# Retention and two MLPs on one core: in-weight stores moved to block 1, ring requests one by one, evacuations ahead of units

## The chip, the cores and the metric

The kernel runs on 1 core of one Trainium2 chip. The metric is the device time of one execution in microseconds (us). TensorE (PE) does the matmuls into PSUM, ScalarE (ACT) and VectorE (DVE) evacuate PSUM and convert operands, GpSimd (POOL) takes a few elementwise operations, and SyncE (SP) issues almost all DMAs. Every engine takes its own instructions in the order in which the program wrote them.

## The reference

```python
# retention, B=4, H=8, S=768, D=64
for t in range(S):
    state = gamma * state + outer(k[t], v[t])
    y[t] = (1 / sqrt(D)) * q[t] @ state
x = y.transpose(0, 2, 1, 3).reshape(3072, 512)
# first MLP, 512 -> 2048 -> 512
h = maximum(x @ w_in, 0.0)
x = h * h @ w_out
# second MLP, 512 -> 1536 -> 512
xn = x / sqrt(mean(x * x) + 1e-6) * rms_g
g = xn @ w_gate
out = (g / (1 + exp(-g)) * (xn @ w_val)) @ w_out
```

The weights come as 64-bit floats, everything else as 32-bit floats.

## The kernel before, in words

**Arithmetic.** A 32-bit operand is held as a high part (rounded to the matmul's own format) and a low part (what the rounding left). A product is three matmuls: high by high, high by low, low by high (`mm3`, lines 243 to 246, and `proj`, line 269). Where a large product allows it, a scheme of seven products in place of eight is used (P1 to P7): `Out` for the output projections, `pair` for the second MLP's first layer. Its seven weight combinations are "units" of 512 KB (128 partitions by 1024 values).

**Stages.** The 3072 tokens are six tiles of 512. Tile 0 goes through `block1(0, ...)`, tile 1 through `block1(1, ...)` (called block 1 below): for each of 16 steps f a projection with the in-weight f, squared ReLU, and the product with the out-weight f. Tiles 2 and 3 go through the first paired phase: `in_phase(xs, ...)` (line 1064; per step f two half steps t = 0, 1, one per tile, each a projection into `ph[t]`, evacuated by ACT with L394 and L395), then `out_1.run`. Tiles 4 and 5 do the same in the second paired phase (`in_phase(xs2, ...)`, line 1144, and `out_2.run`). Then the second MLP runs in three super-steps s of two tiles, each six pairs (`pair`, line 633) and an `out_3.run`.

**Retention beside it.** The chunks of the retention are computed in "visits" (`visit`, `after_visit`): every second step of block 1 and of the first paired phase a visit computes one chunk, its result goes through `xh` (ACT) and `xl` (DVE) into the operand of a later tile, and the loads of `vnt`, `knt`, `qnt`, `kTt` for the chunk after the next are issued on SP. POOL scales `qnt` and `vnt`.

**Weight conversion.** `tick` (line 221) converts one 128x512 piece of 64-bit weights per call: ACT's L203 (`magnitude`) writes a buffer `f` of three, one piece ahead; DVE's L208 and L209 (`convert`) finish it, and `fetch_to` loads the raw piece (512 KB) that comes three later. The next tick's `finish2` stores a gate or value piece to DRAM (`wq<-f`, L181, 256 KB), or splits an out-weight piece and leaves the store of its units to `later`. `more_steps(W2_SOON)` at step 15 of block 1 opens the first 25 of the second MLP's 36 pieces; the rest follow in the second paired phase. `stores()` issues what was appended to `later`.

**Ring and units.** In the second paired phase and in the output projections weights come through a ring of seven buffers, refilled in the order of `stream`. The in-weights of the second paired phase are read back from `wi`, which the first paired phase stores (line 1042). The first seven loads are issued together behind step 13 (lines 1055 to 1058). In super-step 0 of the second MLP the units are made in place: `make_unit(n, k)` (line 592) reads quarters of the gate and value weights (`quarter`, loaded from `wq`), casts with ACT and DVE into `own[k]`, loads the next pair's quarter into the one just freed, and appends the unit's store `wu` to `later`; the next `make_unit` begins with `stores()`.

**Order of a pair.** `both(k, acc, ...)` is a product of 12 matmuls. P1, P6, P7 and P4 go into `main` (`ph` or `pb`, by turns), P5 and P3 into `pa`, P2 into `pr`. `take` copies an accumulator with ACT (L111 in the trace), `add` adds it with DVE (L107), `act2` is SiLU on ACT (L628) and a product on DVE (L629). P7 writes `main` only after `take(p6, main)`, and P4 only after `add(p5, main)`. The units are made between these steps, in the order in which the program has them.

Of the kernel before, what the change touches and what calls it, by code (L numbers as in the profile page):

```python
# [9 lines left out]
F32 = mybir.dt.float32  # L10
F32R = mybir.dt.float32r
# [28 lines left out]
AHEAD = 5  # L40
EARLY = 24
MORE_AT = 15
W2_SOON = 25
OPEN_AT = 12
PREP_IN = 10

P2, P1, P5, P6, P7, P3, P4 = range(7)
# [10 lines left out]
def retention_then_two_mlps(  # L58
    ctx: ExitStack, tc: tile.TileContext, qT, kT, kn, vn, w1i, w1o, w2g, w2v, w2o, rmsg, tri, qdec, vdec, sdec, dec, out
):  # L60
    nc = tc.nc
# [10 lines left out]
    wi = [dram.tile([128, 2, 512], F32, name=f"wi{f}") for f in range(NF1)]  # L72
# [11 lines left out]
    def slot(name, dt=F32):  # L84
        return wp.tile([128, 2, 512], dt, tag="w", name=name)
# [13 lines left out]
    def split(dst_h, dst_l, src, el):  # L99
        nc.scalar.copy(dst_h, src)  # L100
        low(el, dst_l, src, dst_h)

    def sub(out_, a, b):
        nc.vector.tensor_tensor(out=out_, in0=a, in1=b, op=ALU.subtract)

    def plus(out_, a, b):
        nc.vector.tensor_tensor(out=out_, in0=a, in1=b, op=ALU.add)  # L107

    def take(dst, acc):
        for m in range(2):  # L110
            nc.scalar.copy(dst[:, m], acc[m])  # L111

    def add(dst, acc):
        for m in range(2):
            plus(dst[:, m], acc[m], dst[:, m])

    def units(t):
        return t.rearrange("p i (l n) -> p i l n", l=2)

    W = {}  # L120
# [17 lines left out]
    def keep_units(to, f, w):  # L138
        q, r, c = f // 4, f % 4 // 2, f % 2
        for k, h in ((P1, 0),) if r == 0 else ((P2, 0), (P4, 1)):  # L140
            nc.sync.dma_start(units(to[q][k])[:, c], w.bitcast(F32)[:, :, h * HALF:(h + 1) * HALF])
# [73 lines left out]
    later = []  # L215

    def stores():
        while later:
            later.pop(0)()
# [19 lines left out]
    def more_steps(n):  # L239
        upto[0] = min(upto[0] + n, len(steps))  # L240
        fetch_to(at[0] + 2)
# [128 lines left out]
    ring, own, stream, ring_at = [], [], [], [0]  # L370

    def load_unit(i):
        if i < len(stream):
            nc.sync.dma_start(ring[i % 7].bitcast(F32), stream[i])

    def next_unit():
        i = ring_at[0]
        ring_at[0] += 1
        return ring[i % 7]

    def unit_done():
        load_unit(ring_at[0] + 6)
# [204 lines left out]
    def load_quarters(n, *which):  # L587
        if n < NPR:
            for r, h in which:
                nc.sync.dma_start(quarter[r, h], w2q[n][:, r, h])  # L590

    def make_unit(n, k):
        stores()
        if n >= NPR:
            return
        a11, a12, a21, a22 = (quarter[r, h] for r in range(2) for h in range(2))
        u = units(own[k])

        def put(src):
            split(u[:, :, 0, :], u[:, :, 1, :], src, nc.vector)  # L600

        if k == P5:
            plus(mix, a21, a22)
            put(mix)
            sub(a21, a11, a21)
        elif k == P6:
            sub(mix, mix, a11)
            put(mix)
            sub(a11, a12, mix)
            load_quarters(n + 1, (0, 1))  # L610
        else:
            put({P1: a11, P2: a12, P3: a11, P7: a21, P4: a22}[k])
            if k in (P3, P7, P4):
                load_quarters(n + 1, {P3: (0, 0), P7: (1, 0), P4: (1, 1)}[k])
        later.append(lambda: nc.sync.dma_start(wu[n][k], own[k].bitcast(F32)))

    def product(acc, u, k, m, start):
        xh, xl = X[k]
        for c in range(2):
            wc = slice(c * 128, (c + 1) * 128)  # L620
            mm3(
                acc, u[:, m, 0, wc], u[:, m, 1, wc], xh[:, c], xl[:, c], start and c == 0, c == 1,
                skip_group_check=True,
            )

    def act2(g, v, a):
        t = tp.tile([128, TB], F32, tag="t0", name="t")
        nc.scalar.activation(t, g, AF.Silu)  # L628
        nc.vector.tensor_tensor(out=a, in0=v, in1=t, op=ALU.mult)  # L629
# [3 lines left out]
    def pair(s, n, first, second):  # L633
        p1, p5, p6 = part[:3]
        a0, a1 = (act[n % 2][t][n // 2] for t in range(2))
        main = (ph, pb)[n % 2]

        def both(k, acc, start):
            u = units(own[k] if s == 0 else next_unit())
            for m in range(2):  # L640
                product(acc[m], u, k, m, start)
            if s:
                unit_done()
            elif n == NPR - 1:
                load_unit(ORDER.index(k))

        def make(n, k):
            if s == 0:
                make_unit(n, k)

        both(P2, pr, True)
        make(n, P7)
        both(P1, main, True)
        make(n, P3)
        make(n, P4)
        take(p1, main)
        add(p1, pr)
        first()
        act2(p1[:, 0], p1[:, 1], a0[:, 0])
        both(P5, pa, True)  # L660
        take(p5, pa)
        make(n + 1, P2)
        make(n + 1, P1)
        both(P6, main, False)
        take(p6, main)
        second()
        make(n + 1, P5)
        both(P7, main, False)
        make(n + 1, P6)
        add(p5, main)  # L670
        act2(p5[:, 0], p5[:, 1], a1[:, 1])
        both(P3, pa, False)
        add(p6, pa)
        act2(p6[:, 0], p6[:, 1], a1[:, 0])
        both(P4, main, False)
        act2(main[0], main[1], a0[:, 1])

    with tc.manual_schedule():
# [299 lines left out]

        def keep_out(f):
            keep_units(uo, f, W[("o", f)])  # L980

        xs = []
        made = all_units()
# [7 lines left out]
        def early1(f):  # L991
            if f == MORE_AT:
                more_steps(W2_SOON)
            if f > MORE_AT:
# [44 lines left out]
        def after1(f, t):  # L1039
            nonlocal at_chunk  # L1040
            if t == 0:
                nc.sync.dma_start(wi[f], W[("i", f)].bitcast(F32))
                stores()
                tick()
                if f and f % 2 == 0:
                    decay_v(at_chunk + 1, nc.gpsimd)
                    decay_q(at_chunk + 2, nc.gpsimd)
                    at_chunk += 1
            elif f % 2:
                kv = visit(at_chunk, pa, True)  # L1050
                after_visit(at_chunk, sink2(at_chunk), kv)
            elif f % 2 == 0:
                tick()
            make_some()
            if f == 13 and t == 0:
                ring.extend(slot(f"ring{n}", F32R) for n in range(7))
                for n in range(7):
                    load_unit(n)
            if (f, t) in ((14, 1), (15, 0), (15, 1)):
                n = (f - 14) * 2 + t - 1  # L1060
                out_1.hi(n)
                out_1.lo(n)
# [44 lines left out]
        out_2 = Out(NQ, act, pair2)  # L1107
# [15 lines left out]
        def after2(f, t):  # L1123
            if t == 1:
                unit_done()
            if f < OPEN_AT and t == 0:
                stores()
                tick()
            if t == 1 and 3 <= f < 7:
                if f == 3:  # L1130
                    yn.extend(big(f"yn{t_}") for t_ in range(2))
                h, t_ = ((1, 0), (0, 0), (0, 1), (1, 1))[f - 3]
                nc.sync.dma_start(yn[t_][:, 2 * h:2 * h + 2, :], ys[t_][:, 2 * h:2 * h + 2, :])
            if f == 5 and t == 0:
                prep[0] = prep_x(0, {(h, t_): yn[t_][:, 2 * h:2 * h + 2, :] for h in range(2) for t_ in range(2)}, True)
                next(prep[0])
            if (f, t) in ((14, 1), (15, 1)):
                out_2.hi(f - 14)
                out_2.lo(f - 14)

        def w_of2(f):
            return next_unit()

        in_phase(xs2, w_of2, after2, between2)
        out_2.hi(2)
        next(prep[0], None)
        while back:
            background()
# [62 lines left out]
        for s in range(NS):  # L1211
# [5 lines left out]
            for p in range(NPR):  # L1217
# [7 lines left out]
                def first():  # L1225
                    background()
                    if p == 0:
                        background()
                    if p == NPR - 1:
                        for n in range(2):  # L1230
                            out_3.hi(n)
                            out_3.lo(n)
                        next(coming, None)
                        next(coming, None)

                def second():
                    if p == 0 and due:
                        sums(pb[1])
                        background()
                    if p == NPR - 1:  # L1240
                        out_3.hi(2)
                        next(coming, None)
                        next(coming, None)
# [86 lines left out]
```

## Time and profile before

| | before |
|---|---|
| median of three runs | 1146.3 us (1145.23 to 1146.66) |
| the profiled execution's own time | 1146.94 us |
| its span, first to last instruction | 1145.2 us |
| PE busy | 1112.7 us (97%) |
| DVE busy | 713.8 us (62%) |
| ACT busy | 561.0 us (49%) |
| POOL busy | 46.0 us (4%) |
| mean granted clock of PE | 0.993 |

Busy time is the union of an engine's instructions; issuing a DMA doesn't count. "Idle before" an instruction is put down to whatever ended it last. The DMA share is the mean busy share of the core's 16 DMA engines. A matmul of 512 columns shows 0.39 us, as matmuls overlap. Times in the rows are us from the span's start. The stages lie at: block 1 from 143 to 242, first paired phase to 374, `out_1` to 453, second paired phase to 541, `out_2` to some 618, super-step 0's pairs from there to beyond 720.

### The profile page before, as it was taken

The numbers are of one execution on the slowest core, as the hardware profiler recorded it, in microseconds if no ns is written. First come the engines' busy times: TensorE is split into PE (matmuls) and PEld (weight loads), VectorE is DVE, ScalarE is ACT, GpSimd is POOL, SyncE is SP. The second block draws the span as 40 slices with busy tenths as digits, with TensorE's granted clock in tenths as the row PEclk, the third lists the DMA queues.
The fourth block names the chain that finished last, engine by engine and source line by source line (L and its number), as shares of the span: only waits on it lengthen the run. The fifth ranks groups of instructions, "written<-read, shape, count | busy, mean of one in ns | idle before, by whom it ended". The sixth has DMA issues, their size and how long they took to land.

```text
span 1145.2 us, 15762 instructions
## 1 busy us (share of the span) xinstructions
PE 1112.7 (97%) x5962; PEld 909.0 (79%) x5962; DVE 713.8 (62%) x962; ACT 561.0 (49%) x918; POOL 46.0 (4%) x39
## 2 busy tenths in 40 slices
PE   9999999999977999999999999999999999999998
PEld 7788888887765788888888787888888888888887
DVE  6877337767842774442977676888343788333585
ACT  4776445557644542665546444454323454323442
POOL 0000122112110000000000000000000000000000
PEclk9999999999999899999999999999999999999999
DMA  9943445699999467874556568666656666555563
GB/s 359 342 157 112 148 129 195 222 368 340 331 390 368 159 208 259 299 254 153 203 193 239 216 237 322 224 205 231 211 200 242 234 209 232 211 195 194 193 212 118
DMA packets 96411, 266.68 MB, mean 233 GB/s; under 512 B 10168, under 2 KB 27472, under 8 KB 96336
## 3 DMA queue, kind: packets, MB, share of 16 engines
q1 hardware_dynamic: 95760, 265.47, 65.3%
q8 instruction: 47, 0.77, 0.3%
q10 hardware_dynamic: 576, 0.20, 0.1%
q14 instruction: 28, 0.23, 0.1%
HBM read 190.65 MB, written 74.99 MB: 232 GB/s over the span
## 4 chain that ended last, share of the span: by engine, by line
PE 85%; DMA 7%; DVE 3%; ACT 3%; issue 1%; SPq 0%; ACTq 0%; DVEq 0%
PE ph L276 17%; PE ph L244 8%; PE ph L245 8%; PE ph L246 8%; PE pa L244 7%; PE pa L246 6%; PE pa L245 6%; PE pb L244 4%; PE pb L246 4%; PE pb L245 4%; PE pr L245 3%; PE pr L244 3%; PE pr L246 3%; DMA up<-wps 2%; DMA wi<-w_i 1%; PE pr L773 1%
## 5 line engine op out<-in xcount | busy, mean ns | idle before, releaser
L276 PE MATMUL ph<-xh,w_i 128*128 128x512 f32 x512 | 167.7, 395 | 11.6 <-ACT act L394 10.3
L435 ACT CAST o<-act 128x1024 fp32r<-128x1024 f32 x101 | 105.7, 1052 | 99.4 <-PE ph L246 44.0
L97 DVE TENSOR_TENSOR o<-act,o 128x1024 fp32r<-128x1024 f32 x101 | 122.6, 1220 | 35.6 <-ACT o L435 35.6
L276 PEld LDWEIGHTS ph<-xh,w_i 128*128 128x128 f32 x512 | 96.7, 189 | 35.9 <-ACT act L394 12.9
L276 PE MATMUL ph<-xl,w_i 128*128 128x512 f32 x256 | 100.0, 392 | 0.0
L244 PE MATMUL ph<-o,ring 128*128 128x512 f32 x228 | 88.7, 389 | 0.0
L245 PE MATMUL ph<-o,ring 128*128 128x512 f32 x228 | 88.7, 389 | 0.0
L246 PE MATMUL ph<-o,ring 128*128 128x512 f32 x228 | 88.7, 389 | 0.0
L276 PE MATMUL ph<-xh,ring 128*128 128x512 f32 x256 | 79.3, 390 | 0.0
L628 ACT ACTIVATE t<-part 128x512 f32<-128x512 f32 x54 | 34.1, 632 | 67.3 <-DVE part L107 67.3
L107 DVE TENSOR_TENSOR part<-pr,part 128x512 f32<-128x512 f32 x36 | 24.9, 692 | 65.7 <-ACT part L111 65.7
L244 PE MATMUL ph<-xop,ring 128*128 128x512 f32 x144 | 57.2, 397 | 2.9 <-ACT part L111 2.0
L111 ACT COPY part<-ph 128x512 f32<-128x512 f32 x50 | 29.1, 588 | 62.7 <-PE ph L246 62.6
L244 PE MATMUL pb<-xop,ring 128*128 128x512 f32 x144 | 56.4, 392 | 2.1 <-ACT part L111 1.5
L245 PE MATMUL ph<-xop,ring 128*128 128x512 f32 x144 | 56.8, 394 | 0.0
L246 PE MATMUL ph<-xop,ring 128*128 128x512 f32 x144 | 56.6, 393 | 0.0
L276 PEld LDWEIGHTS ph<-xl,w_i 128*128 128x128 f32 x256 | 48.5, 189 | 9.7
L276 PEld LDWEIGHTS ph<-xh,ring 128*128 128x128 f32 x256 | 48.1, 188 | 10.1 <-issue 0.2
L246 PE MATMUL pb<-xop,ring 128*128 128x512 f32 x144 | 56.1, 389 | 0.0
L245 PE MATMUL pb<-xop,ring 128*128 128x512 f32 x144 | 56.0, 389 | 0.0
L246 PE MATMUL pa<-xop,ring 128*128 128x512 f32 x144 | 56.0, 389 | 0.0
L245 PE MATMUL pa<-xop,ring 128*128 128x512 f32 x144 | 56.0, 389 | 0.0
(209 smaller groups left out, 2512.8 us busy)
## 6 DMA issues: line engine op xcount, KB each, us to landing
ring<-wu SPq DMA_DIRECT2D x84, 512.0 KB, 3.3
ring<-up SPq DMA_DIRECT2D x63, 512.0 KB, 4.3
ring<-uo SPq DMA_DIRECT2D x56, 512.0 KB, 3.3
wu<-ring SPq DMA_DIRECT2D x42, 512.0 KB, 4.0
raw<-w1i SPq DMA_DIRECT2D x16, 512.0 KB, 6.6
raw<-w1o SPq DMA_DIRECT2D x16, 512.0 KB, 7.8
uo<-made SPq DMA_DIRECT2D x16, 512.0 KB, 5.5
wi<-w_i SPq DMA_DIRECT2D x16, 512.0 KB, 8.8
```

The lines of the kernel that those rows point to most:

```text
L97: eng.tensor_tensor(out=dst_l, in0=src, in1=dst_h.bitcast(F32), op=ALU.subtract)
L107: nc.vector.tensor_tensor(out=out_, in0=a, in1=b, op=ALU.add)
L111: nc.scalar.copy(dst[:, m], acc[m])
L244: nc.tensor.matmul(acc, ah, bh, start=start, stop=False, **more)
L245: nc.tensor.matmul(acc, ah, bl, start=False, stop=False, **more)
L246: nc.tensor.matmul(acc, al, bh, start=False, stop=stop, **more)
L276: nc.tensor.matmul(h, w[:, a, k * 128:(k + 1) * 128], x[b][k], start=n == 0, stop=n == len(order) - 1)
L435: nc.scalar.copy(h, src)
L628: nc.scalar.activation(t, g, AF.Silu)
L773: nc.tensor.matmul(a[heads[h ^ SWAP[p]], :], vv[:, p, h, :], P[:, h, p, :], start=(p == 0 or two and p == 2), stop=(c < B and p in (1, 3)) ...
```

## The change

The 16 stores of in-weights to `wi` move from the first paired phase (`after1`) to block 1 (`keep_out`). Two fewer conversions are opened early (23 in place of 25); so the tick at half step (14, 1) goes, and the second paired phase gets two more ticks, at (2, 1) and (6, 1). The seven first ring buffers are taken and requested one per half step, from (12, 0) to (15, 0). In the second paired phase the high and low parts of `out_2`'s first operands are made one half step or more earlier, in the last two steps. In `make_unit` the loads of quarters are appended to `later` in front of the unit's store. In `pair` the units of P4 (this pair), P1, P5 and P6 (next pair) are made later, behind `take` and `add` of the accumulators.

```diff
-W2_SOON = 25
+W2_SOON = 23
@@ make_unit
             sub(a11, a12, mix)
-            load_quarters(n + 1, (0, 1))
+            later.append(lambda: load_quarters(n + 1, (0, 1)))
         else:
             put({P1: a11, P2: a12, P3: a11, P7: a21, P4: a22}[k])
             if k in (P3, P7, P4):
-                load_quarters(n + 1, {P3: (0, 0), P7: (1, 0), P4: (1, 1)}[k])
+                later.append(lambda: load_quarters(n + 1, {P3: (0, 0), P7: (1, 0), P4: (1, 1)}[k]))
@@ pair
         make(n, P3)
-        make(n, P4)
         take(p1, main)
         add(p1, pr)
         first()
         act2(p1[:, 0], p1[:, 1], a0[:, 0])
         both(P5, pa, True)
+        make(n, P4)
         take(p5, pa)
         make(n + 1, P2)
-        make(n + 1, P1)
         both(P6, main, False)
         take(p6, main)
+        make(n + 1, P1)
         second()
+        both(P7, main, False)
+        add(p5, main)
         make(n + 1, P5)
-        both(P7, main, False)
-        make(n + 1, P6)
-        add(p5, main)
         act2(p5[:, 0], p5[:, 1], a1[:, 1])
         both(P3, pa, False)
         add(p6, pa)
+        make(n + 1, P6)
         act2(p6[:, 0], p6[:, 1], a1[:, 0])
@@ keep_out (block 1)
             keep_units(uo, f, W[("o", f)])
+            nc.sync.dma_start(wi[f], W[("i", f)].bitcast(F32))
@@ after1 (first paired phase)
             if t == 0:
-                nc.sync.dma_start(wi[f], W[("i", f)].bitcast(F32))
                 stores()
@@
-            elif f % 2 == 0:
+            elif f % 2 == 0 and f < 14:
                 tick()
             make_some()
-            if f == 13 and t == 0:
-                ring.extend(slot(f"ring{n}", F32R) for n in range(7))
-                for n in range(7):
-                    load_unit(n)
+            if 2 * f + t >= 24 and len(ring) < 7:
+                n = len(ring)
+                ring.append(slot(f"ring{n}", F32R))
+                nc.sync.dma_start(ring[n].bitcast(F32), stream[n])
@@ after2 (second paired phase)
-            if f < OPEN_AT and t == 0:
+            if f < OPEN_AT and (t == 0 or f in (2, 6)):
                 stores()
                 tick()
@@
-            if (f, t) in ((14, 1), (15, 1)):
-                out_2.hi(f - 14)
-                out_2.lo(f - 14)
+            if (f, t) in ((13, 1), (14, 1)):
+                out_2.hi(f - 13)
+                out_2.lo(f - 13)
+            if f == 15:
+                if t:
+                    out_2.lo(2)
+                out_2.hi(2 + t)
@@ behind in_phase(xs2, ...)
-        out_2.hi(2)
```

## Rows read from the trace of the kernel before

**Rows 1.** The page: busy us, share of the span and instructions, by engine.

```profile
PE 1112.7 (97%) x5962; PEld 909.0 (79%) x5962; DVE 713.8 (62%) x962; ACT 561.0 (49%) x918; POOL 46.0 (4%) x39
```

**Rows 2.** PE's waits (total us, times, longest): whole span; last line, 245 to 308.

```profile
PE ph L276 <- ACT act L394: 10.3, 5, 4.0
PE pr L244 <- DVE xl L97: 9.4, 1, 9.4
PE ph L244 <- ACT part L111: 2.0, 1, 2.0
PE pb L244 <- ACT part L111: 1.5, 1, 1.5
...
PE ph L244 <- DVE part L107: 0.9, 2, 0.6
PE pb L244 <- DVE part L107: 0.6, 2, 0.4
...
PE pr L245 <- DVE o L97: 0.6, 1, 0.6
...
PE ph L276 <- ACT act L394: 4.3, 3, 1.9
```

**Rows 3.** By stretch: length, busy PE, PEld, DVE, ACT, POOL; clock, DMA share, GB/s.

```profile
143.00:200.00 57.00, 57.00 (x455) 46.27 (x454) 29.82 (x49) 26.89 (x56) 14.34 (x11) 1.00 0.49 162
200.00:245.00 45.00, 45.00 (x298) 36.83 (x297) 34.27 (x56) 23.15 (x48) 6.98 (x5) 1.00 0.76 268
245.00:307.00 62.00, 58.46 (x456) 46.04 (x454) 46.16 (x75) 42.12 (x88) 13.88 (x10) 1.00 0.92 349
307.00:365.00 58.00, 50.91 (x344) 40.30 (x344) 23.92 (x44) 26.89 (x50) 7.26 (x6) 0.97 1.03 383
365.00:375.00 10.00, 0.63 (x6) 0.50 (x2) 4.24 (x6) 6.63 (x11) 0.00 (x0) 0.68 0.59 222
...
453.00:541.00 88.00, 88.00 (x402) 72.47 (x402) 36.48 (x49) 54.76 (x86) 0.00 (x0) 1.00 0.71 242
```

**Rows 4.** ACT's waits from 245 to 375 us (total us, times, longest).

```profile
ACT f L203 <- DMA wq<-f: 32.6, 6, 9.2
ACT st L794 <- DVE st L107: 8.5, 4, 3.5
```

**Rows 5.** In order of time (start, us, what, idle before and releaser), around 322 us.

```profile
321.76 0.66 ACT L203 ACTIVATE f<-raw 128x512 f32<-128x512 f32 x1 [9.16 <-DMA wq<-f]
...
323.48 0.50 PE L276 MATMUL ph<-xh,w_i 128*128 128x512 f32 x1 [3.98 <-ACT act L394]
```

**Rows 6.** In order of time, the end of the first paired phase.

```profile
368.30 0.66 ACT L203 ACTIVATE f<-raw 128x512 f32<-128x512 f32 x1 [8.95 <-DMA wq<-f]
...
373.61 0.63 ACT L100 CAST xh<-pr 128x256 fp32r<-128x256 f32 x2
...
374.00 0.76 DVE L97 TENSOR_TENSOR xl<-pr,xh 128x256 fp32r<-128x256 f32 x2 [0.19 <-ACT xh L100]
```

**Rows 7.** By stretch, as in rows 3, three short ones behind waits of PE.

```profile
324.00:328.00 4.00, 4.00 (x12) 3.09 (x12) 3.97 (x9) 2.79 (x7) 0.00 (x0) 0.57 1.08 317
374.00:379.00 5.00, 4.52 (x11) 3.56 (x12) 4.50 (x7) 3.08 (x4) 0.00 (x0) 0.51 0.12 40
712.00:717.00 5.00, 4.35 (x12) 3.44 (x13) 3.28 (x5) 2.04 (x5) 0.00 (x0) 0.66 0.98 399
```

**Rows 8.** SP's queue, its longest waits in block 1, 143 to 245 us.

```profile
SPq L705 <- PE pr L773: 38.7, 5, 10.7
```

**Rows 9.** DMA issues, count, size, median us to landing: block 1; then 245 to 375.

```profile
uo<-w_o SPq DMA_DIRECT2D x19, 256.0 KB, 4.6
...
wq<-f SPq DMA_DIRECT2D x12, 256.0 KB, 7.8
```

**Rows 10.** In order of time, ACT in two pairs of super-step 0.

```profile
645.11 1.28 ACT L327 ACT_TABLE_LOAD   x1
...
711.50 0.62 ACT L100 CAST ring<-q 128x512 fp32r<-128x512 f32 x1 [2.41 <-DMA q<-wq]
```

## The prediction

> **What bounds the kernel now.** I read the busy times first: TensorE (PE) is busy 97% of the span [rows 1], so a change can only win PE's idle time or time at a lowered clock. The list of who PE waited for comes second [rows 2]: 10.3 us for the first MLP's activations (five waits), 9.4 us in a single wait for `xl`, then some 5.0 us in the pairs of the second MLP and 0.6 us at its `o`. That is 25.3 us in all; the rest of PE's idle time is start and end, which the diff leaves alone. Third, the table by stage [rows 3] says where and why. Block 1 (143 to 245 us) has no idle PE, with the DMA engines at a share of 0.49 and then 0.76. The paired phase of the first MLP (245 to 375) holds all of the 19.7 us of the first two waits, and there the DMA share is 0.92 and 1.03 at 349 and 383 GB/s: full. Fourth, who ScalarE (ACT) waits for in that phase [rows 4]: six waits, 32.6 us, of L203 for the store `wq<-f`. L203 writes the next buffer `f` of three, so it needs the store of an older one to land; ACT takes its instructions in order, so the evacuation L394 that frees PE's accumulator stands behind it. One instance in order of time [rows 5]: ACT resumes L203 at 321.76 after 9.16 us idle, L394 follows, PE starts again at 323.48 after 3.98 us. The end of the phase is the same case with PE one step further [rows 6]: L203 at 368.30 after 8.95 us, and only then the casts `xh` and lows `xl` for which PE waited the 9.4 us. So the bound of this stage is a saturated set of DMA queues, seen by PE through ACT's order.
>
> The clock adds to it. PE's granted clock fell to the lower of its two levels (1.2 of 2.4 GHz) behind three such waits [rows 7]. A mean of 0.57 over 4 us is 3.4 us at half speed, 1.7 us lost. A mean of 0.51 over 5 us, less the 0.5 us in which PE was still idle, is 4.4 us, 2.2 us lost. A mean of 0.66 over 5 us is 3.4 us, 1.7 us lost. That is 5.6 us, 3.9 of it in the paired phase. Idle and clock together: 30.9 us, the most that the change could win.
>
> **The change, part by part.** (1) The stores `wi<-w_i`, 16 of 512 KB, 8.4 MB, leave `after1` and go to `keep_out`, so to block 1. Two conversions move to the second paired phase: each loads 512 KB and stores 256 KB, 1.6 MB. By the rates of [rows 3], 62 us at 349, 58 at 383 and 10 at 222 GB/s, the phase moves 46.1 MB today; 36.1 are left. If PE's waits vanish the phase lasts about 111 us, so 325 GB/s, 85% of the 383 that its full stretch reached. Block 1 goes from 57 us at 162 and 45 at 268 GB/s (21.3 MB in 102 us) to 29.7 MB, 291 GB/s, 76%. On SP's queue the 16 stores are ahead of the visit's loads, but there SP waits 38.7 us in five waits for PE to release `vnt` [rows 8], and the new issues mostly fall before such a wait. I cost them at nothing there; what hides them is that wait. Without it (the last 15 us of block 1) each takes 1.4 us of the queues at 383 GB/s; two or three fall there, which may start the phase up to 4 us late in its loads.
>
> A price beside a page: the Trainium skill, "DMA: Bandwidth & Descriptors", section Specifications, gives about 358 GB/s of HBM per core, by which 36.1 MB would need 101 of those 111 us and little would be won on latency. This trace ran 383 GB/s over 58 us [rows 3], above that figure, and the measurement decides; the sum goes by 383.
>
> How late will stores land below saturation? The nearest row is block 1, where a 256 KB store lands in 4.6 us at the median, against 7.8 us for `wq<-f` in the phase [rows 9]. The store for a buffer needed at one conversion can be issued two conversions earlier, at least two projections before. A projection is 12 matmuls; 402 in the 88.0 us of the second paired phase [rows 3] make 2.6 us of it, two are 5.3 us, so at 4.6 us L203 no longer waits. The bounds are a wait as now (gain 0) and none (gain all). I sit near the lower latency. Of the five waits of 10.3 us, three with 4.3 us lie before 308 [rows 2]; the other two belong to this store, 3.98 [rows 5] and the 2.0 that remain, together 6.0 us: I take 5.2 and keep 0.8. The three before 308 go mostly with ACT waiting for VectorE's state update, 8.5 us in four waits [rows 4], which the change doesn't touch: 1.0 us of 4.3 is won, as loads come sooner; bounds 0 and 4.3.
>
> (2) The end of the phase. The second conversion of step 14 is gone and 23 conversions need no new `f` from step 15 on, so L203 stands no more ahead of the last evacuations. What is late next is the phase's own chain: two casts `xh` of 0.63 us together and the first `xl`, half of 0.76 [rows 6], with handovers about 1.2 us. Of 9.4 us 8.2 are won; bounds 4 (the latency halves) and 8.4. The seven first ring loads, spread over seven half steps, are 3.7 MB that no longer stand in one lump in front of these stores; SP issues each without PE waiting. I cost them at nothing: the first is issued some 20 us before `out_1` reads it.
>
> Clock in the phase: with no long wait it stays up; 3.5 of 3.9 us won, 0.4 kept, as a wait of 1.2 us may still lower it. Bounds 1.7 and 3.9.
>
> (3) Two conversions more in the second paired phase, at half steps 2 and 6. There PE is busy 88.0 of 88.0 us, ACT 54.8, VectorE 36.5, the DMA share 0.71 [rows 3]. Each adds one L203 of 0.66 us [rows 5] to ACT, two instructions to VectorE and 0.8 MB: covered by 33 us of ACT's idle time; 0, at worst 2 us if ACT waits for a store there. `out_2.hi` and `lo` one half step earlier remove the 0.6 us of PE for `o` [rows 2].
>
> (4) Pairs of the second MLP, first super-step. `add(p5, main)` now comes before the units of P5 and P6, `take(p6)` before the unit of P1. PE's four waits for VectorE's `part`, 0.9 and 0.6 us [rows 2], are `add(p5)` behind those units: all 1.5 won. The wait of 2.0 us (ph, ACT) is `take(p6)` behind a cast that waited 2.41 us for a quarter [rows 10]: won, with the 1.7 us of clock behind it. The wait of 1.5 us (pb, ACT) stays: it comes from two table loads of 1.28 us on ACT [rows 10] ahead of the same evacuations, and the cast of P4 now stands there in place of that of P1. So 1.5 + 2.0 + 1.7 = 5.2 us; bounds 2 and 6.7. Quarter loads put on `later` are issued by the next `make_unit`. Relative to the unit stores SP's order is the same; only the quarter behind P6 is moved past other DMAs, in the fifth pair past four line loads of 512 KB, 2.1 MB or 5.5 us at 383 GB/s. It is read by the unit of P2 after P5, three products of 2.6 us later, and that cast is ahead of `take(p6)`: margin about 2 us. P4's unit, made a product later, is needed three products (8 us) after.
>
> The sum: 5.2 + 1.0 + 8.2 + 3.5 + 0.6 + 5.2 = 23.7 us. The profiled execution took 1146.94 us for a span of 1145.2, and becomes 1123.2 us; it stood 0.6 above the median, so the median goes from 1146.3 to **1122.6 us**.
>
> **Rivals.** *The queues stay late* (the page's 358 GB/s, or bursts that a mean of 85% hides): half of (1), (2) and the phase's clock is won, 0.5 × (5.2 + 1.0 + 8.2 + 3.5) + 5.8 = 14.8, so 1131.5 us. For it: the first stretch of the phase was at 0.92 and its traffic is cut by only 8 of the 16 stores. Against it: 383 GB/s was reached. *The pairs win nothing*, because the casts wait for quarters that come later: 18.5 us, 1127.8. For it: the 2.41 us wait on a quarter is there now. Against it: the evacuations no longer stand behind most casts. *All is won*, VectorE's waits too: 30.9 less the 1.2 us chain, 29.7, so 1116.6. *Slower*: the in-weight stores in block 1 delay the loads of `qnt` and `vnt`, which SP issues behind them, and PE waits at each visit. The place is the eight visits of block 1 and the eight of the phase. The price: the 23.7 us won are lost from 1.5 us a visit on, and 2 us at each gives 32, so 1155 us. It decides when a load lands some 8 us later than now, since SP's wait of 10.7 us [rows 8] shows how early in its visit's period (111 us by eight visits, 14 us) a load goes out; two stores per period are 2.7 us of queue time. So it is unlikely. That the stores are not in block 1 after all is not possible: `keep_out` runs there at every step.
>
> **How the numbers follow.** Forecast 0.60 (1118 to 1127), queues late 0.17, pairs nothing 0.08, all won 0.10, slower 0.05. The measurement of this kernel tells about 0.2%, 2.3 us, from no change. Of the late queues 0.02 reach that far. So faster 0.93, same 0.02, slower 0.05. The range from 1115 to 1134 takes in all but the slower case and the far ends of the late queues.
>
> **What would show it.** In the profile after: DMA share of the paired phase below 0.95, block 1 above 0.7 with no PE wait in it; ACT's waits for `wq<-f` under 8 us in sum; PE's wait before `out_1` between 1 and 2 us; clock 1.00 around it; in the pairs only the wait with the table loads left. I am wrong if the phase still shows a DMA share over 1.0, if PE waits in block 1 for POOL or a DMA, or if PE waits for a `ring` unit in the pairs.

## The result, and the profile after

| | before | after |
|---|---|---|
| median | 1145.8 us (1145.2 to 1146.7) | 1126.9 us (1125.4 to 1128.0) |
| ratio, 95% interval | | 0.9833 (0.9816 to 0.9850) |
| the same two kernels on another chip: median, ratio | 1146.2 us | 1124.1 us, 0.9799 (0.9785 to 0.9812) |
| profiled execution: own time, span | 1146.94, 1145.2 us | 1127.32, 1125.5 us |

The change wins 18.9 us in the first comparison and 22.2 us in the second. The forecast was 23.7 us (1122.6 us), the range 1115 to 1134. Why the two comparisons differ is told below; the profile shown here is of the first.

Whom PE waited for over the whole span, as in [rows 2], and last the part from 245 to 308 us:

```profile
PE ph L276 <- ACT act L394: 4.7, 4, 2.0
PE ph L244 <- ACT part L111: 2.4, 1, 2.4
PE pb L244 <- ACT part L111: 1.5, 1, 1.5
...
PE pr L244 <- DVE xl L97: 0.9, 1, 0.9
...
PE pb L244 <- DVE part L107: 0.2, 1, 0.2
...
PE ph L276 <- ACT act L394: 2.7, 3, 1.1
```

Of the 25.3 us that seven rows held before, 9.7 are left. The wait before `out_1` fell from 9.4 to 0.9 us and the waits for activations from 10.3 to 4.7. The wait for ACT's `part` in `ph`, 2.0 us before, is not gone: it is 2.4.

The table by stage (length; busy us of PE, PEld, DVE, ACT, POOL; clock; DMA share; GB/s), to be set against [rows 3]; the last two lines are the stretches of low clock, as in [rows 7]:

```profile
143.00:200.00 57.00, 57.00 (x455) 46.25 (x454) 29.59 (x49) 27.07 (x56) 14.29 (x11) 1.00 0.65 235
200.00:245.00 45.00, 45.00 (x298) 36.84 (x297) 33.81 (x57) 23.39 (x49) 7.71 (x5) 1.00 0.86 313
245.00:307.00 62.00, 59.20 (x459) 46.71 (x458) 44.70 (x75) 43.55 (x91) 13.18 (x10) 1.00 0.84 304
307.00:355.00 48.00, 46.02 (x301) 36.72 (x300) 26.76 (x42) 26.40 (x49) 7.98 (x6) 0.96 1.00 372
355.00:365.00 10.00, 9.08 (x65) 7.12 (x65) 7.79 (x10) 7.51 (x11) 0.00 (x0) 1.00 0.19 66
...
442.00:530.00 88.00, 88.00 (x401) 72.31 (x400) 42.37 (x57) 59.28 (x91) 0.00 (x0) 1.00 0.73 253
...
320.00:324.00 4.00, 4.00 (x13) 3.08 (x12) 3.97 (x9) 3.39 (x8) 0.00 (x0) 0.58 1.05 408
...
692.00:697.00 5.00, 4.45 (x13) 3.50 (x14) 1.92 (x3) 1.60 (x4) 0.00 (x0) 0.66 1.02 413
```

Block 1 took the stores (share 0.65 and 0.86 in place of 0.49 and 0.76) with PE busy in every one of its 102 us. The second paired phase took the two conversions with PE busy 88.00 of 88.00 us. But the first paired phase still has a full stretch: a share of 1.00 at 372 GB/s from 307 to 355. What ACT waited for from 245 to 375 (total us, times, longest), and in the fence behind it how a store of `f` landed there (count, size, median us), against [rows 4, 9]:

```profile
ACT f L203 <- DMA wq<-f: 12.9, 4, 7.2
ACT st L794 <- DVE st L107: 9.9, 4, 3.7
```

```profile
wq<-f SPq DMA_DIRECT2D x11, 256.0 KB, 7.0
```

The store lands in 7.0 us, hardly sooner than the 7.8 before. There are four waits for it in place of six: 8.95 of the 32.6 us belonged to one of the two conversions that are gone [rows 6], and the other 23.7 us fell to 12.9. The longest of the four still stops PE, for 1.98 us, with a stretch of low clock behind it (in order of time):

```profile
317.79 0.66 ACT L203 ACTIVATE f<-raw 128x512 f32<-128x512 f32 x1 [7.15 <-DMA wq<-f]
...
319.51 0.50 PE L276 MATMUL ph<-xh,w_i 128*128 128x512 f32 x1 [1.98 <-ACT act L394]
```

The end of the phase, in order of time (start, us, what, idle before and what ended it), against [rows 6]:

```profile
357.29 0.60 ACT L394 ACTIVATE act<-ph 128x512 f32<-128x512 f32 x1 [0.52 <-PE ph L276]
...
358.91 0.65 ACT L100 CAST xh<-pr 128x256 fp32r<-128x256 f32 x2 [0.36 <-PE pr L782]
359.32 0.76 DVE L97 TENSOR_TENSOR xl<-pr,xh 128x256 fp32r<-128x256 f32 x2 [1.28 <-ACT xh L100]
...
359.80 0.50 PE L244 MATMUL pr<-oh,ring 128*128 128x512 f32 x1 [0.92 <-DVE xl L97]
```

No L203 stands here any more: ACT waits for PE (0.52 us before L394), not the other way round, and the chain of `xh` and `xl` is all that is left. And the fifth pair of super-step 0, with the issues of the line loads and of one quarter load ahead of it:

```profile
677.45 2.28 SPq L1224 DMA_DIRECT2D line<-ys  x4
...
682.05 0.32 SPq L590 DMA_DIRECT2D q<-wq  x1
...
691.40 0.62 ACT L100 CAST ring<-q 128x512 fp32r<-128x512 f32 x1 [3.38 <-DMA q<-wq]
691.92 1.06 ACT L111 COPY part<-ph 128x512 f32<-128x512 f32 x2
...
692.55 0.69 PE L244 MATMUL ph<-xop,ring 128*128 128x512 f32 x1 [2.44 <-ACT part L111]
```

A cast that waits for a quarter still stands ahead of `take(p6)`; now it is that of P2's unit. Its quarter was issued at 682.05 us, behind the lines, and landed at 691.3, 9.3 us later.

### The profile page after: what moved, and what is told of

Its sections match the earlier page's. It is cut to its first block, busy times and chain, and to the rows that moved or that the text cites. A ratio compares the mean times of both kernels' runs of the same rounds, so it can differ in the third digit from the quotient of the medians.

```text
span 1125.5 us, 15733 instructions
## 1 busy us (share of the span) xinstructions
PE 1108.9 (99%) x5962; PEld 907.7 (81%) x5962; DVE 714.2 (63%) x962; ACT 560.0 (50%) x918; POOL 46.7 (4%) x39
## 4 chain that ended last, share of the span: by engine, by line
PE 87%; DVE 4%; DMA 4%; ACT 3%; issue 1%; SPq 1%; ACTq 0%; DVEq 0%
PE ph L276 18%; PE ph L244 8%; PE ph L245 8%; PE ph L246 8%; PE pa L244 7%; PE pa L245 6%; PE pa L246 6%; PE pb L244 4%; PE pb L246 4%; PE pb L245 4%; PE pr L244 3%; PE pr L245 3%; PE pr L246 3%; PE pr L773 1%; PE ph L749 1%
## 5 line engine op out<-in xcount | busy, mean ns | idle before, releaser
L244 PE MATMUL ph<-o,ring 128*128 128x512 f32 x228 | 88.7, 389 | 0.0
L244 PE MATMUL ph<-xop,ring 128*128 128x512 f32 x144 | 56.9, 395 | 2.4 <-ACT part L111 2.4
L244 PE MATMUL pb<-xop,ring 128*128 128x512 f32 x144 | 56.3, 391 | 1.7 <-ACT part L111 1.5
```

The lines of the kernel that those rows point to most:

```text
L244: nc.tensor.matmul(acc, ah, bh, start=start, stop=False, **more)
```

## The experiments

A ratio is to the kernel before on the same chip, with its 95% interval. "The changed kernel" stands at 0.9833 in its first comparison and 0.9799 in the second.

**The pairs.** One quarter load out of four is issued at once again:

```diff
             sub(a11, a12, mix)
-            later.append(lambda: load_quarters(n + 1, (0, 1)))
+            load_quarters(n + 1, (0, 1))
```

> The changed kernel with one of its four quarter loads (the one behind the unit of P6) issued at once again, ahead of the four line loads of the fifth pair. Theory: the wait of 2.4 us for take(p6) in the fifth pair and the 1.7 us of low clock behind it come from this one load, which landed 9.3 us after its issue; it lands within 3 us, both go, and the time is about 4.1 us under that of the changed kernel, some 1122.8 us. Rival: the other quarters, which come behind the lines in either kernel, are as late; then the wait only moves to the next product (P7 or P4 behind the cast of P1's unit), and the time is within 1 us of the changed kernel's.

Measured: 1128.6 us, 0.9835 (0.9820 to 0.9849): nothing won. In order of time:

```profile
697.66 0.62 ACT L100 CAST ring<-q 128x512 fp32r<-128x512 f32 x1 [7.86 <-DMA q<-wq]
698.31 0.69 DVE L97 TENSOR_TENSOR ring<-q,ring 128x512 fp32r<-128x512 f32 x1 [9.98 <-ACT ring L100]
698.92 1.28 DVE L107 TENSOR_TENSOR part<-ph,part 128x512 f32<-128x512 f32 x2
...
699.66 0.79 PE L244 MATMUL ph<-xop,ring 128*128 128x512 f32 x1 [5.04 <-DVE part L107]
```

The theory that one load was at fault falls. `take(p6)` is in time now, but the cast of P1's unit waits 7.86 us for its own quarter, DVE waits for that cast, and `add(p5, main)` stands behind DVE's low part of that unit: PE waits 5.0 us at P4 in place of 2.4 at P7, and a clock of 0.58 from 699.6 to 706 us costs 2.7 us more. This second quarter was issued at 689.12 us, behind the lines as well, and landed 8.5 us later.

The new order of the pairs alone, put on the kernel before (the hunk of `pair` of the change). The kernel that ran lacks the hunk of `make_unit`, so its quarter loads go out at once, though the recorded expectation speaks of deferred ones:

> The kernel before with the new order of the pairs and the deferred quarter loads alone. Theory: the four waits for add(p5), 1.5 us, go; the wait in the fifth pair stays at 2.0 to 2.5 us with its 1.7 us of clock; the first paired phase is as before. So 1.0 to 2.0 us faster than before, 0.1 to 0.2%. The prediction's own step said 5.2 us for it (about 1140.6). Rival: the new order takes nothing from PE at all, as other waits step in: within 0.5 us of before.

Measured: 0.9991 (0.9982 to 1.0001), 0.9 us and not clear of nothing. The four waits of 1.5 us go, down to 0.2; the fifth pair's wait does not stay at 2.0 but moves to P4 and grows to 4.1, and the clock of 0.56 from 716.8 to 723 us behind it costs 2.7 us, against 1.7 before:

```profile
PE ph L244 <- DVE part L107: 4.1, 1, 4.1
PE pb L244 <- ACT part L111: 1.5, 1, 1.5
```

So the order alone, which was to win the 5.2 us, loses more in the fifth pair by its rows (2.1 us of wait, 1.0 of clock) than it wins in the small waits (1.3). Order and deferred loads together ran only inside the changed kernel; the rows there are in the table further below. Next, the cause that both runs point to: the line loads ahead of the quarters. Two loads of `rr`, 256 KB each, move with them.

```diff
             for p in range(NPR):
-                if p == NPR - 2 and s + 1 < NS:
-                    lines = {(h, t): slot("line") for h in range(2) for t in range(2)}
-                    ...
                 def second():
+                    nonlocal coming
+                    if p == NPR - 2 and s + 1 < NS:
+                        lines = {(h, t): slot("line") for h in range(2) for t in range(2)}
+                        ...
```

> The changed kernel with the four line loads and the two loads of rr of the fifth pair issued in second(), behind all four quarter loads of that pair, in place of at its start. Theory: what makes the fifth pair wait is that every quarter comes behind 2.1 MB of lines, whichever of the casts stands first; then no wait over 0.5 us is left there, the clock stays at its higher level, and the time is 4 us (0.35%) under that of the changed kernel, a ratio to the kernel before of about 0.980. Rival: the queues are full there from the stores of units alone; then a wait of 1.5 us or more stays at P7 or P4 in the fifth pair and the gain is under 1.5 us. A second rival: the lines now come too late for the sixth pair, and the first product of super-step 1 waits for an operand.

Measured: 1120.8 us, 0.9775 (0.9762 to 0.9788), the lowest time of all, and 3.3 us under the kernel with the ring loads in one lump (below), which took the changed kernel's time and ran on the same chip. In the whole list of PE's waits no row of `ph` L244 is left, and super-step 1 starts without a wait. P2's quarter goes out at 681.85 us, nearly as in the changed kernel, and its cast does not wait for it now (first fence). The stretches of the fifth pair (second fence, columns as in [rows 3]):

```profile
687.33 0.62 ACT L100 CAST ring<-q 128x512 fp32r<-128x512 f32 x1
```

```profile
676.00:682.00 6.00, 6.00 (x28) 4.99 (x27) 5.17 (x9) 2.77 (x7) 0.00 (x0) 1.00 0.39 158
682.00:688.00 6.00, 6.00 (x28) 4.96 (x27) 4.75 (x9) 4.45 (x9) 0.00 (x0) 1.00 0.83 263
688.00:694.00 6.00, 6.00 (x28) 4.98 (x27) 3.16 (x5) 1.83 (x4) 0.00 (x0) 1.00 1.02 405
694.00:700.00 6.00, 6.00 (x28) 4.97 (x27) 4.70 (x8) 2.77 (x6) 0.00 (x0) 1.00 1.01 315
```

The queues are still full for the second half, with the lines in them, but what waits behind the lines are stores that PE does not wait for, and PE is busy throughout. The same edit on the kernel before:

> The kernel before with the line loads of the fifth pair issued in second(), nothing else. Theory: in the old order too the quarters are late only because of the lines; the wait of 2.0 us in the fifth pair and the 1.7 us of clock behind it go, 3.5 to 4 us faster than before, ratio 0.9968, while the four waits for add(p5), 1.5 us, stay. Rival: the old order needs the new one as well, and less than 1 us is won.

Measured: 1142.9 us, 0.9965 (0.9953 to 0.9978), 3.3 us of the 3.5 to 4 expected. No wait for ACT's `part` is left in `ph`; the fifth pair waits 0.27 us for DVE, and the four small waits stay (0.6, 0.35, 0.27 and 0.27 us):

```profile
PE ph L244 <- DVE part L107: 1.1, 3, 0.6
...
PE pb L244 <- DVE part L107: 0.6, 2, 0.3
```

So the 3.7 us of [rows 2, 7] that the prediction gave to the order of evacuations belonged to the place of the line loads, in the old order as in the new.

**The first paired phase.** The stores of in-weights moved, nothing else (`wi[f]` from `after1` to `keep_out`, 25 conversions and the lump of ring loads as before):

> The kernel before with the 16 stores of in-weights moved to block 1 and nothing else (25 conversions, ring loads in one lump). Theory of the queues: 8.4 of 46.1 MB leave the phase, stores land sooner, and the wait before out_1 falls from 9.4 to 3 or 4 us, PE's waits for activations from 10.3 to about 5; 10 to 13 us faster than before, 1133 to 1136 us. Rival: what counts is the two conversions that ended the phase; then the wait before out_1 stays above 7 us and the gain is under 6 us.

Measured: 1135.8 us, 0.9898 (0.9883 to 0.9913), 11.6 us. PE's waits for activations fall to 4.5 us, the wait before `out_1` to 4.8:

```profile
PE pr L244 <- DVE xl L97: 4.8, 1, 4.8
PE ph L276 <- ACT act L394: 4.5, 4, 1.6
```

Two conversions fewer, nothing else (`W2_SOON = 23`, no tick at (14, 1), ticks at (2, 1) and (6, 1) of the second phase):

> The kernel before with two conversions fewer in the first paired phase and two ticks more in the second, nothing else. Theory now: the wait before out_1 is the last conversions' alone; it falls from 9.4 us to 1 or 2 us and its clock loss of 2.2 us goes, while PE's waits for activations stay at 9 to 11 us; 9 to 11 us faster than before, ratio 0.991. Rival (the queues decide the end too): the wait before out_1 stays at 4 us or more, 4 to 6 us faster.

Measured: 0.9929 (0.9915 to 0.9942), 7.7 us; less than the 9 to 11 expected. The wait before `out_1` falls only to 3.2 us, between the two views (first fence). What is left of it is not a conversion: the last L203, at 354.79 us, waits for nothing. The chain runs through a store of in-weights (second fence, in order of time). SP issues it behind the seven ring loads, it lands 10.1 us later, and DVE's `ol`, which comes ahead of `xl`, waits for it:

```profile
PE ph L276 <- ACT act L394: 8.5, 5, 3.8
PE pr L244 <- DVE xl L97: 3.2, 1, 3.2
```

```profile
347.28 7.14 SPq L374 DMA_DIRECT2D ring<-uo  x7
354.70 0.32 SPq L1042 DMA_DIRECT2D wi<-w_i  x1
...
364.94 1.22 DVE L97 TENSOR_TENSOR ol<-act,oh 128x1024 fp32r<-128x1024 f32 x1 [4.11 <-DMA wi<-w_i]
```

The changed kernel without its first part (`wi[f]` stored in `after1` again):

> The changed kernel with the stores of in-weights back in the first paired phase. Theory of the queues: DMA share 1.0 all through the phase, PE waits for activations 8 to 12 us, the wait before out_1 3 to 5 us since no conversion stands ahead of it; 8 to 12 us slower than the changed kernel, 1135 to 1139 us. Rival (the two conversions count, not the stores): within 3 us of the changed kernel.

Measured: 0.9861 (0.9847 to 0.9876). That is 3 us above the changed kernel by the first comparison and 7 by the second, so neither view holds in full. By the profile each holds for its half: PE's waits for activations are back at 11.1 us, as the queues' view had it; the wait before `out_1` is 0.9 us all the same, which that view had put at 3 to 5.

```profile
PE ph L276 <- ACT act L394: 11.1, 9, 3.8
...
PE pr L244 <- DVE xl L97: 0.9, 1, 0.9
```

Moving the stores wins the waits inside the phase. At its end either part alone wins about half or more (9.4 to 4.8 or 3.2 us), and it takes the two conversions and one thing more, the stores moved or the ring loads spread, to come down to 0.9: either keeps a store of in-weights from standing behind the lump of ring loads. A wait of one profile is not exact, though: the kernel with the new order alone has the first paired phase of the kernel before, and shows 7.6 us before `out_1` in place of 9.4. The seven ring loads in one lump again:

```diff
-            if 2 * f + t >= 24 and len(ring) < 7:
-                ...
+            if f == 13 and t == 0:
+                ring.extend(slot(f"ring{n}", F32R) for n in range(7))
+                for n in range(7):
+                    load_unit(n)
```

> The changed kernel with its seven first ring loads in one lump behind step 13 as before. Theory (the prediction cost this edit at nothing): within 1 us of the changed kernel, as nothing that PE needs is stored behind the lump once no conversion ends the phase. Rival: the lump delays the last stores wq by some 5 us, and the wait before out_1 grows from 0.9 to 3 us or more.

Measured: 1124.2 us, 0.9801 (0.9788 to 0.9814), the wait before `out_1` 0.9 us: the same as the changed kernel's second comparison. Once the stores are moved and no conversion ends the phase, asking for the ring one by one is worth nothing, as forecast.

Four buffers `f` in place of three:

```diff
-        cf = rctx.enter_context(tc.tile_pool(name="cf", bufs=3))
+        cf = rctx.enter_context(tc.tile_pool(name="cf", bufs=4))
```

> The changed kernel with four buffers f in place of three. Theory: the wait of 2.0 us that is left near 317 us, and the 1.7 us of low clock behind it, are L203 waiting for the store of a buffer that lands some 8 us after its issue; with a fourth buffer that store has one conversion more, ACT's waits for wq fall from 12.9 us to under 3, and the time is 3 to 4 us (0.3%) under that of the changed kernel. Rival: the raw loads are as late, so ACT waits for raw in place of wq and PE's waits for activations stay at 4 to 5 us.

Measured: 0.9795 (0.9776 to 0.9814). ACT's waits for `wq` are gone, and waits for the raw loads take their place:

```profile
ACT f L203 <- DMA raw<-w2v: 7.1, 2, 5.7
...
ACT f L203 <- DMA raw<-w2g: 4.0, 1, 4.0
```

That is 11.1 us in place of 12.9; PE's waits for activations are 3.8 us, just under the rival's 4 to 5, and the time is not below that of the changed kernel's second comparison (0.9799) by more than the noise. So the rival holds in the main: it is the queues, not the number of buffers, that is short there.

**The clock, and the best version.** The changed kernel once more:

> The changed kernel, unedited, beside the three below on one chip. Theory: the low clock behind a wait of about 2 us is a matter of how the wait falls, so this kernel's time varies with whether it shows none, one or two stretches of 1.7 us loss: a ratio to the kernel before between 0.980 and 0.985. Rival: its low clock is there in every execution, and the ratio is 0.983 again.

Measured: 0.9799, at the low end of the theory. Its profile has the same wait near 320 us, 2.00 us long (in order of time, first fence), and no low clock behind it; the fifth pair's wait was 0.9 us, again at full clock (by stretch, second fence):

```profile
320.73 0.50 PE L276 MATMUL ph<-xh,w_i 128*128 128x512 f32 x1 [2.00 <-ACT act L394]
```

```profile
318.00:325.00 7.00, 5.00 (x23) 3.79 (x22) 4.75 (x10) 5.92 (x12) 0.00 (x0) 1.00 1.05 402
688.00:695.00 7.00, 6.13 (x27) 4.75 (x26) 1.61 (x3) 2.21 (x4) 0.00 (x0) 1.00 1.04 412
```

So a wait of 2 us sometimes lowers the clock and sometimes doesn't. Two stretches that lose 1.7 us each and 1.5 us of the fifth pair's wait, 4.9 us in all, are more than enough for the 3.2 us between the two profiles' spans (1125.5 and 1122.3) and the 3.3 us between the two comparisons. The other executions agree: in the first comparison all four have a mean clock of 0.997 or 0.998, in the second three of five have 1.000, and the slowest of these five, 1125.4 us, has 0.998. The two comparisons ran on two chips, so a part that belongs to the chip is not excluded. Lines in `second()` and four buffers together:

> The changed kernel with the lines in second() and four buffers f. Theory: the gains add as far as they are different waits: PE's waits for activations 3.8 in place of 5.0 us, none in the fifth pair, clock 1.00 throughout; 1 us under the lines in second() alone, ratio 0.9765. Rival: four buffers let raw loads queue up and give nothing once the clock stays up; the same within 0.5 us.

Measured: 1121.0 us, 0.9772 (0.9759 to 0.9786): no distance from lines in `second()` alone, as the rival had it. And the unit of P4 later still:

```diff
         both(P5, pa, True)
-        make(n, P4)
         take(p5, pa)
         ...
         take(p6, main)
+        make(n, P4)
         make(n + 1, P1)
```

> As the one before, and the unit of P4 made behind take(p6) in place of ahead of take(p5). Theory: the wait of 1.5 us in the second pair is ACT's evacuations behind two table loads and the casts; with P4's cast behind them it falls by one cast, 0.5 us, to 0.9 to 1.0 us, and the time by as much. Rival: another cast or the quarter of P4, issued later, takes its place; no change, or a new wait in the first pairs.

Measured: 0.9782 (0.9769 to 0.9795). The wait behind the table loads falls by 0.5 us to 1.0, as the theory had it, and the rival holds as well: in the sixth pair PE now waits 1.8 us for `add(p5, main)`, which DVE takes behind its part of the moved unit and four operations on lines. No time is won.

```profile
PE pb L244 <- DVE part L107: 1.8, 1, 1.8
PE pb L244 <- ACT part L111: 1.5, 2, 1.0
```

The best version is the changed kernel with the lines in `second()`, 1120.8 us; four buffers beside it give the same time.

## Why the prediction was right, and where not

| step | forecast | profile after | second comparison's profile |
|---|---|---|---|
| two waits for stores of `f`, 6.0 us | 5.2 | 4.0 (one of 1.98 left) | 4.0 |
| three waits before 308, 4.3 us | 1.0 | 1.6 (2.7 left) | 1.1 (3.2 left) |
| end of the phase, 9.4 us | 8.2 | 8.5 (0.9 left) | 8.5 |
| clock in the phase, 3.9 us | 3.5 | 2.2 | 3.9 |
| `o` of `out_2` | 0.6 | 0.6 | 0.6 |
| pairs: `add(p5)` | 1.5 | 1.3 | 1.2 |
| pairs: `take(p6)` and its clock | 3.7 | -0.4 | 2.8 |
| sum | 23.7 | 17.8 | 22.1 |

The spans differ by 19.7 us in the first; the 1.9 us that the sum lacks are not put down to a row, since waits are counted from modelled ends of matmuls.

**Right:** that the bound was a full set of DMA queues, seen by PE through ACT's order; where the gain would come from; that block 1 and the second paired phase had the room (PE busy throughout both); the end of the phase, 0.9 us against 1.2; the ring's request at nothing; the wait behind the table loads, unchanged at 1.5 us.

**Lucky in part, the total.** In the first comparison the pairs bring 0.9 us of their 5.2, which is what the rival that the pairs win nothing had said (1127.8 us, chance 0.08; measured 1126.9). The forecast's range takes that in, so the total alone does not bear out the step. In the second comparison's profile the pairs bring 4.0 us.

**Wrong, the fifth pair.** The step said that the wait for `take(p6)` is won. It saw that P2's cast still stands ahead of it, with a quarter that the change itself puts behind the lines, and gave that quarter 5.5 us of queue time (2.1 MB at 383 GB/s) with a margin of 2 us. The load took 9.3 us, in which the DMA engines moved 3.0 MB at 325 GB/s: the loads of `rr` and the stores of units are in the same queues. The runs with one load moved, with the order alone and with the lines moved, on either kernel, show that the line loads, with the loads of `rr` that go with them, delay the quarters behind them (9.3 us for P2's, 8.5 for P1's), and that an order of evacuations only chooses which product waits.

**Mis-sized, the latency in the paired phase.** The forecast put the store's landing near block 1's 4.6 us, from a mean load of 85% of the full rate. The mean was near (311 GB/s over 245 to 365 by the table, against 325), but not even: 304 GB/s first, then 372 at a share of 1.00. The stores of gates and values, from 309 us, and the ring loads, from 336, all lie in the second stretch; the store lands in 7.0 us there, and one PE wait of 2 us is left. Two of the prediction's signs show it: ACT's waits for `wq<-f` were to stay under 8 us and are 12.9, and the DMA share of the phase, 0.85 in the mean, reaches the 1.0 that was to be a sign of being wrong. So the rival of late queues had a part in it, though far from half. The first three waits, which a slow VectorE was to keep, lost more than forecast.

The part in the prediction that gave the end of the phase to the missing conversions holds for most of it: they alone take 6.2 of the 9.4 us. Moving the stores alone takes half of that wait as well, and what the conversions leave is a late store of in-weights, a term that the prediction did not have there. Its traffic for block 1 was a little high: three of the 16 stores are issued before 143 us, and the stretch to 245 runs at some 270 GB/s, not 291.

## What to carry to other kernels

Where an engine's in-order queue puts an evacuation behind something that waits for a DMA, ask first what fills the DMA queues at that moment: here moving the evacuation ahead only passed the wait to the next step, while moving the bulk transfer behind the small urgent ones took it away. A mean load below capacity did not tell the latency; take the load of the stretch in which the urgent transfer is issued, and a transfer's own issue-to-landing time behind a burst. Ask of each moved load what it now stands behind, and price that by a landing, not by a rate.

## What the runs showed of the hardware that was not expected

Waits of PE of nearly one length had different results: the 2.0 us before in the fifth pair and 1.98 us after at 319 us were followed by 3.4 us at the lower level of the clock, and 2.00 us at that same place in another execution of the changed kernel by none. A longer wait need not lower it either: behind the 3.22 us before `out_1` with two conversions fewer the clock stayed at 1.00 (first line below). Each stretch of 3.4 us costs 1.7 us, so two of them are 3.4 us between two executions of one program. While the line loads were in the queues, these were busy at less than their best rate: the 6 us from 677 of the changed kernel show a share of 0.91 at 293 GB/s (second line), and with the lines in `second()` the stretch from 694 shows 1.01 at 315, where the changed kernel's stretch from 692 shows 1.02 at 413. Which transfers make the difference is not shown.

```profile
366.00:372.00 6.00, 5.45 (x24) 4.50 (x25) 5.46 (x7) 1.90 (x2) 0.00 (x0) 1.00 0.29 100
...
677.00:683.00 6.00, 6.00 (x28) 4.95 (x27) 5.31 (x10) 2.66 (x5) 0.00 (x0) 1.00 0.91 293
```
